# A fused transformer block on one core: the bias add moves to GpSimd, two more sums are kept, some leftover rows are copied side by side, and the order is new

## The chip, the cores and the metric

The kernel runs on one NeuronCore of a Trainium2 chip. The metric is the device time of one execution in microseconds (us). Before the change it is 149.14 us as the median of three runs (148.47 to 150.26).

## What is computed

The reference normalizes x of 2048 rows and 640 columns (bf16) along its columns, sends the result xn through two branches, and adds both to x:

```python
xn = _layernorm(x, axis=-1)
X = rfft2(xn.astype(float32)) * (w_r + 1j * w_i)
y = irfft2(X, s=(S, D)).astype(bfloat16)          # branch A, S = 2048, D = 640
h = gelu(xn @ w1 + b1)                            # w1: 640 x 1536
return x + y + (h @ w2 + b2)                      # w2: 1536 x 640
```

## The kernel before, in words

The rows of x are held as 16 chunks, one row of each group of 16 in each chunk, with 128 partitions and 640 columns a chunk. Everything of the kernel is one function, which registers operations by name with a class `Plan` (line 108 on): each has an engine, the buffers that it reads and writes, and the operations it must follow. The order is not left to a scheduler at run time: a string `ORDER` (line 251 on) lists all 887 operations as `engine:name`, and each engine works through its own part of that list strictly in order. A string `SLOTS` gives every buffer its slot, PSUM banks among them. `Plan.sync` (line 167) then works out which semaphores each operation must wait for. So an operation that waits holds up all that stands behind it on its engine. The five lists are: `sp` (SyncE, which only issues DMAs, transposes by DMA among them), `pe` (TensorE), `act` (ScalarE), `dve` (VectorE) and `pool` (GpSimd). A `gate` in the code concerns only how a list was made; the machine does not wait for it.

The stages and their names (a number behind the letter is a chunk c, a pair of chunks, a group of chunks or a block):

- **Start.** `idle0` are 38 small products on zeros, until the first chunk is there. `st`, `ag`, `ve`, `rs`, `nm` (lines 521 to 553) make statistics and xn of a chunk on VectorE; from chunk 2 on the power of -1/2 (`rs`, line 532) is on GpSimd. `tp` and `tc` transpose the first four chunks by TensorE and a copy, `td` (line 559) the other twelve by DMA. `table0` and `table1` load ScalarE's tables, `b1mm` and `b1cp` turn b1 into a column.
- **First layer of branch B.** `h{block}.{column tile}.{part}` are products of w1 with the transposed xn into PSUM, `ge` the gelu on ScalarE into gT. Chunks go in blocks of 1, 1, 2, 2, 2, 4 and 4.
- **Second layer.** For each chunk, 12 products of 384 columns and 12 of 256 (parts .0, .3, .6, .9). A chunk in `KEEP` (line 246: 1, 2, 4, 5, 7, 8, 10, 11) has them under the name `k`, and `kk` (line 796, VectorE) adds x + b2 and keeps the sum in float32 where the transposed xn lay. The other chunks have them as `l`, which stay in their PSUM bank until the last product of branch A (`fin`, line 803) is added to the same bank. `os` (line 806, VectorE) adds what is kept, or x + b2, and writes the bf16 result, which `out` stores.
- **b2.** `xs` (lines 602 to 608) adds the row b2, copied to all partitions, to x in place, two chunks at a time (`SUMS` = 2, line 245), eight adds of 1280 columns on VectorE. It must follow the normalization of its chunks; `kk` and `os` read its result. The row lies in a buffer that `u` (below) uses later, so each `u` follows all `xs`. The load `bias2` on SP brings it.
- **Branch A on the way in.** `f1` and `f2` (lines 580 and 584) fold the columns of a pair of chunks (even and odd parts) on VectorE, `G` (line 590) is the first step along the rows on TensorE, `gx` its copy to XV. `b0` to `b5` (line 657) are the transform of the columns for a group of 3, 3, 2, 3, 3 and 2 chunks (`GROUPS`); `xb` copies the result out of PSUM. Each `b` takes four PSUM banks, the same four, so b1 waits until both copies of b0 are done. A product here has 160 columns: four with 128 rows for a chunk, and for the 32 leftover rows of each of the four parts four with 32 rows, which use a quarter of the array each (function `width`, line 644).
- **Middle.** `c` (line 722) and `d` (line 731) are the second step along the rows and its inverse, in 16 groups of 32 products with 32 rows and columns each; `y` copies, `m` and `z` multiply with the filter W (VectorE), `u` copies to U. `vt` (line 705) are 16 transposes by DMA from U to XV, issued by SP.
- **The way back.** `e0` to `e5` (line 756) are the mirror of b, for the same groups; each reads all 16 transposes' results and the table `i`. Their weights are slices of XV with a step of 16 elements. `yo` copies out, `y2` and `yf` unfold the columns (VectorE), then `fin` and `os`.

In the order before, part .0 to .9 of l3 and the first part of l0 stand between the last d and e0 on TensorE, and the rest of l0 behind e0.

Of the kernel before, what the change touches and what calls it, by code (L numbers as in the profile page):

```python
# [107 lines left out]
class Plan:  # L108
# [58 lines left out]
    def sync(self):  # L167
# [8 lines left out]
        for o in self.ops:  # L176
            o.waits = [d for d in set(o.deps) if d.dma or d.eng != o.eng or o.eng != "pe"]
# [68 lines left out]
KEEP = (1, 2, 4, 5, 7, 8, 10, 11)  # L246
# [5 lines left out]
sp:x0 dve:warm0 act:bias1 pool:id0 pool:wpad dve:eps5 pool:id1 pe:idle0 sp:x1 act:table0 pool:xbpad2a pool:mhalf pool:xbpad0a pool:xbpad0b  # L252
pool:xbpad1b sp:w1_00 pool:xbpad1a pool:xbpad2b sp:w1_01 sp:w1_02 dve:st0.0 sp:x2 dve:st0.1 sp:w1_03 dve:st1.0 sp:w1_04 dve:ag0 dve:st1.1 sp:w1_10
act:sq0 dve:rs0 dve:ag1 sp:w1_11 dve:nm0 act:sq1 pe:b1mm dve:nm0.3 act:table1 sp:w1_12 dve:rs1 pe:tp0.3 dve:nm1 pe:tp0.0 sp:w1_13 pe:idle1 dve:tc0.0
pe:tp1.0 sp:w1_14 dve:f10.1 pe:h0.0.0 dve:f10.0 sp:x4 pe:h0.1.0 act:tc1.0 pe:h0.0.1 pe:h0.1.1 sp:x6 dve:f20.11 pe:h0.0.2 act:tc0.3 dve:f20.00
pe:h0.1.2 pe:h1.1.0 sp:g act:b1cp pe:h1.1.1 pe:h1.1.2 sp:x8 pe:h1.0.0 dve:st3.0 pe:h1.0.1 pe:h1.0.2 sp:x10 dve:st3.1 pe:h0.0.3 pe:h1.0.3 sp:x12
pe:h1.1.3 dve:ag3 dve:st2.0 pe:h0.0.4 pe:h0.1.3 dve:ve3 pe:h1.0.4 act:ge0.1 dve:st2.1 pe:h0.3.0 pool:rs3 pe:h1.1.4 act:ge1.0 pe:h0.2.0 dve:ag2
act:ge0.0 pe:h0.3.1 dve:ve2 pe:h0.1.4 act:ge1.4 dve:nm3 pe:h0.2.1 pool:rs2 pe:h0.2.2 act:ge0.3 dve:f20.10 pe:h1.3.0 act:ge1.1 pe:h1.3.1 dve:f20.01
pe:h0.3.2 act:ge1.2 dve:nm2 pe:tp3.0 pe:h1.3.2 dve:f11.0 pe:h1.3.3 act:tc3.0 pe:h1.3.4 dve:f11.1 pe:h0.3.3 pe:tp2.0 act:ge0.2 dve:st5.0 pe:h0.2.3
pe:h0.2.4 act:tc2.0 pe:h1.2.0 dve:st4.1 pe:h1.2.1 pe:h0.3.4 dve:st4.0 act:ge1.10 pe:h1.2.2 pe:h1.2.3 act:ge0.11 dve:st5.1 pe:h1.2.4 act:ge1.9  # L260
pe:h2.6.0 dve:ag4 act:ge1.5 dve:ag5 pe:h2.6.3 dve:st7.0 act:ge1.7 pe:h2.7.0 act:ge0.9 dve:ve4 dve:f21.10 pe:h2.2.0 pool:rs4 act:ge1.3 dve:f21.01
act:ge1.11 pe:h2.2.3 dve:st6.1 pe:h2.3.0 act:ge0.4 dve:nm4 act:ge0.5 pe:h2.7.3 act:ge0.10 pe:h2.3.3 dve:st7.1 sp:td4 pe:h2.10.0 act:ge1.8 dve:f21.00
act:ge2.6 pe:h2.10.3 pe:h2.11.0 dve:nm5 act:ge2.7 pe:h2.11.3 dve:st9.1 act:ge1.6 pe:h2.0.0 act:ge0.6 sp:td5 dve:st9.0 pe:G1 act:ge2.10 dve:f21.11
# [60 lines left out]
kps5_0:5 kps5_384:7 fps5_0:0 fps5_384:3 yo2:1 y22:0 yf2:0 eps2:0 os6:0 fps6_0:5 fps6_384:4 os7:1 kps7_0:5 kps7_384:7 fps7_0:2 fps7_384:7 yo3:0 y23:0  # L324
yf3:1 eps3:0 os8:0 kps8_0:4 kps8_384:5 fps8_0:5 fps8_384:7 os9:3 fps9_0:5 fps9_384:3 os10:2 kps10_0:7 kps10_384:4 fps10_0:0 fps10_384:2 yo4:1 y24:0
yf4:0 eps4:0 os11:2 kps11_0:4 kps11_384:7 fps11_0:4 fps11_384:4 os12:0 fps12_0:1 fps12_384:2 os13:1 fps13_0:7 fps13_384:0 yo5:1 y25:0 yf5:0 eps5:0
os14:1 fps14_0:6 fps14_384:4 os15:3 fps15_0:1 fps15_320:3 fps15_480:5
"""


def bass_parallel_sum__spectral_gfnet__dense_activation_gelu__prompt_kernel(
# [20 lines left out]
    K = Plan(nc)  # L352
# [494 lines left out]
```

## Time and profile before

| | us |
|---|---|
| median of three runs | 149.14 (148.47 to 150.26) |
| the profiled execution, its own time | 148.87 |
| its span, first to last instruction | 147.5 |
| TensorE busy (of the span) | 141.7 (96%) |
| VectorE busy | 114.7 (78%) |
| ScalarE busy | 79.3 (54%) |
| GpSimd busy | 7.2 (5%) |

A line such as `PE L410` names the engine and the line of the kernel. Here all products of TensorE but the transposes have line 410, and most copies line 420 (ScalarE) or 421 (VectorE), since helpers record them; they are told apart by what they read and write (`ps<-getab,XV` are the e groups, `ps<-EB,XV` the b groups, `ps<-T,ntab` the d groups, `ps<-xnT,W` the first layer, `ps<-W,gT` the second). In a timeline the first number is the start, the second the length of the run of operations, `x` their number, and the bracket the idle time of the engine before it. Operations overlap by some tens of ns at their ends, so the sum of single lengths is more than the length of a run.

### The profile page before, as it was taken

To read this page: it belongs to the slowest core of one execution; us is meant where nothing else is said; L and a number is where in the kernel's file an instruction comes from. 1 tells how busy PE (TensorE), PEld (TensorE's weight loads), DVE (VectorE), ACT (ScalarE), POOL (GpSimd) and SP (SyncE) were. 2 spreads that over 40 slices of the span, in tenths; PEclk is the share of its full clock that TensorE was granted. 3 is DMA by queue.
4 is the path that set the end of the run, shared out by engine and by line. 5 is a ranking of instruction groups with operands and counts; after the bars stand their busy time and mean duration, and the time that the engine had idled before them with its cause. 6 is when DMAs were issued, how large, how long until landed. Compare 5 with 4: busy or idle time off the path is not lost.

```text
span 147.5 us, 4149 instructions
## 1 busy us (share of the span) xinstructions
PE 141.7 (96%) x1751; PEld 99.8 (68%) x1760; DVE 114.7 (78%) x264; ACT 79.3 (54%) x149; POOL 7.2 (5%) x24
## 2 busy tenths in 40 slices
PE   7999999999999999999999999999899999999993
PEld 7899898886478867455364434446686786667882
DVE  2999999999997555798988999410488789296993
ACT  3659998979755734577795767655242102300000
POOL 2030204112000000000000000000000000000000
PEclk9999999999999999999999999999999999999999
DMA  4999869887999899000007685669001022012225
GB/s 135 306 354 408 142 141 343 145 101 137 293 155 160 221 201 266 16 4 0 7 0 57 126 118 99 103 131 94 2 0 49 0 78 102 5 44 89 89 93 178
DMA packets 29226, 18.40 MB, mean 125 GB/s; under 512 B 20248, under 2 KB 27928, under 8 KB 29080
## 3 DMA queue, kind: packets, MB, share of 16 engines
q1 hardware_dynamic: 29184, 18.14, 54.2%
q8 instruction: 14, 0.23, 0.6%
q14 instruction: 4, 0.03, 0.1%
q10 hardware_dynamic: 24, 0.00, 0.0%
HBM read 10.92 MB, written 2.62 MB: 92 GB/s over the span
## 4 chain that ended last, share of the span: by engine, by line
PE 86%; DMA 4%; ACT 3%; DVE 2%; SPq 2%; issue 1%
PE ps L410 85%; DMA XV<-U 2%; SPq L705 2%; ACT Xb L420 2%; DMA X<-in_A_x_dram 2%; DVE U L521 1%; ACT U L420 1%; PE ps L567 1%; ACT gT L639 0%; DVE T L553 0%; DVE W L806 0%; DVE mv L523 0%; DVE rstd L527 0%
## 5 line engine op out<-in xcount | busy, mean ns | idle before, releaser
L410 PE MATMUL ps<-W,gT 128*128 128x256 bf16 (+3 forms) x396 | 59.3, 296 | 0.0
L410 PE MATMUL ps<-xnT,W 128*128 128x256 bf16 (+2 forms) x411 | 55.5, 286 | 1.2 <-issue 1.1
L410 PEld LDWEIGHTS ps<-W,gT 128*128 128x128 bf16 x396 | 36.9, 98 | 15.4 <-issue 1.2
L410 PEld LDWEIGHTS ps<-xnT,W 128*128 128x128 bf16 x420 | 34.5, 98 | 16.0 <-issue 2.8
L639 ACT ACTIVATE gT<-ps,b1col 128x256 bf16<-128x256 f32 (+2 forms) x84 | 37.6, 524 | 10.3 <-PE ps L410 10.0
L420 ACT ACTIVATE Wf<-ps 128x960 bf16<-128x960 f32 (+1 forms) x8 | 6.7, 869 | 19.2 <-PE ps L410 15.7
L521 DVE BATCH_NORM_STATS2 U<-X 128x6 f32<-128x320 bf16 x32 | 14.1, 473 | 2.1 <-DMA X<-in_A_x_dram 2.1
L420 ACT ACTIVATE T<-ps 128x644 bf16<-128x644 f32 (+2 forms) x17 | 9.3, 580 | 4.7 <-PE ps L410 4.7
L796 DVE TENSOR_TENSOR xnT<-ps,X 128x384 f32<-128x384 f32 (+1 forms) x16 | 7.6, 486 | 4.8 <-PE ps L410 4.8
L806 DVE TENSOR_TENSOR W<-ps,xnT 128x384 bf16<-128x384 f32 (+1 forms) x16 | 7.5, 485 | 4.7 <-PE ps L410 4.5
L420 ACT ACTIVATE XV<-ps 128x1280 bf16<-128x1280 f32 (+1 forms) x8 | 9.6, 1202 | 2.0 <-PE ps L410 2.0
L421 DVE CAST Wf<-ps 128x960 bf16<-128x960 f32 (+1 forms) x4 | 4.3, 1073 | 7.1 <-PE ps L410 7.1
L584 DVE TENSOR_TENSOR T<-T 128x128 bf16<-128x128 bf16 (+1 forms) x32 | 8.9, 315 | 0.1
L806 DVE TENSOR_TENSOR W<-ps,X 128x384 bf16<-128x384 f32 (+3 forms) x17 | 7.6, 465 | 1.7 <-PE ps L410 1.6
L410 PE MATMUL ps<-Wf,htab 128*128 128x384 bf16 (+3 forms) x33 | 8.6, 296 | 0.0
L410 PE MATMUL ps<-getab,XV 32*128 32x160 bf16 (+1 forms) x128 | 7.5, 242 | 0.5 <-DMA XV<-U 0.5
L420 ACT ACTIVATE Xb<-ps 128x960 bf16<-128x960 f32 x5 | 6.2, 1260 | 3.4 <-PE ps L410 3.4
L410 PEld LDWEIGHTS ps<-getab,XV 32*128 32x128 bf16 (+1 forms) x128 | 6.7, 146 | 1.7 <-DMA XV<-U 0.8
L420 ACT ACTIVATE U<-ps 128x512 bf16<-128x512 f32 (+2 forms) x13 | 5.3, 475 | 4.4 <-PE ps L410 4.4
L699 DVE TENSOR_TENSOR T<-T 128x644 bf16<-128x644 bf16 x16 | 7.3, 487 | 0.2
L410 PE MATMUL ps<-EB,XV 32*128 32x160 bf16 (+1 forms) x128 | 7.2, 232 | 0.2 <-ACT Xb L420 0.2
L532 POOL TENSOR_TENSOR rstd<-ve,mhalf 128x2 f32<-128x2 f32 (+1 forms) x8 | 6.1, 758 | 26.6 <-DVE ve L531 26.6
(56 smaller groups left out, 124.6 us busy)
## 6 DMA issues: line engine op xcount, KB each, us to landing
out_dram<-W SPq DMA_DIRECT2D x15, 160.0 KB, 1.8
X<-in_A_x_dram SPq DMA_DIRECT2D x7, 320.0 KB, 5.8
W<-in_B_w_dram SPq DMA_DIRECT2D x10, 192.0 KB, 4.7
W<-in_B_w_dram SPq DMA_DIRECT2D x2, 960.0 KB, 7.0
Wf<-in_A_w_r_dram SPq DMA_DIRECT2D x7, 160.5 KB, 5.5
Wf<-in_A_w_i_dram SPq DMA_DIRECT2D x7, 160.5 KB, 3.8
gtab<-c_G SPq DMA_DIRECT2D x1, 512.0 KB, 7.5
htab<-c_H SPq DMA_DIRECT2D x1, 512.0 KB, 6.1
```

The costliest lines, as they stand in the source:

```text
L410: ins = e.matmul(o_, lhsT=lw, rhs=rh, start=st, stop=sp_, skip_group_check=True)
L420: return e.activation(dst(), src(), ACT.Copy)
L421: return e.tensor_copy(dst(), src())
L521: K.op(f"st{c}.{h}", "dve", lambda e, _, c=c, h=h: e.bn_stats(stats[:, c, 6 * h:6 * h + 6], view(X, c * D + H2 * h, [[1, H2]])), reads=[B_ ...
L532: K.op(f"rs{c0}", "pool", lambda e, _, a=a, b=b: e.tensor_tensor(out=rstd[:, a:b], in0=ve[:, a:b], in1=mhalf[:, a:b], op=ALU.pow), reads=[ ...
L567: ins = e.transpose(psb(tps.slot, [[1, 512]]).bitcast(BF)[:, 128 * j:128 * j + 128], xnv(n, 128 * j, [[1, 128]]), ident)
L584: ring_ops.append(K.op(f"f2{pair}.{k}{i}", "dve", lambda e, _, op=op, x1v=x1v, xfv=xfv, o_=o_, o0=o0, o1=o1, w=w: e.tensor_tensor(out=xfv( ...
L639: K.op(f"ge{bi}.{fc}", "act", lambda e, _, c0=c0, nt=nt, fc=fc, f0=f0, hps=hps: e.activation(gT[:, fc, 128 * c0:128 * (c0 + nt)], psb(hps. ...
L699: return e.tensor_tensor(out=rows, in0=rows, in1=view(TT, TB.slot * 4 * KP + r * KP, [[2 * KP, 2], [1, KP]]), op=op)
L705: K.op(f"vt{q}", "sp", lambda e, _, q=q, qq=qq, U=Us[pair]: e.dma_start_transpose(XV[:, :, 128 * q:128 * q + 128], uv(U, D * qq, [[1, D]]) ...
L796: K.op(f"kk{c}.{o0}", "dve", lambda e, _, kps=kps, c=c, home=home, o0=o0, w=w: e.tensor_tensor(out=home[:, o0 // 128:(o0 + w) // 128], in0 ...
L806: K.op(f"os{c}.{o0}", "dve", lambda e, _, c=c, os_=os_, fps=fps, o0=o0, w=w, kept=kept, home=home if kept else None: e.tensor_tensor(out=( ...
```

## The change

Five things are edited.

1. The eight `xs` are given to GpSimd instead of VectorE.
2. `KEEP` becomes (1, 2, 4, 5, 7, 8, 10, 11, 0, 3). The sums of chunks 0 and 3 are kept where w1 lay, which is free after the whole first layer. Their 16 `l` operations become `k`, and four `kk` are added.
3. For the groups 2 to 5 of the way back, `xr` copies the leftover rows of a group from XV (step 16) to T, chunk by chunk side by side, and the products with 32 rows of that group take their weights from there. There are four such copies, xr2, xr3 and xr4 on ScalarE and xr5 on VectorE.
4. An operation no longer waits on a semaphore for a table load of its own engine.
5. `ORDER` and `SLOTS` are new throughout.

```diff
-            o.waits = [d for d in set(o.deps) if d.dma or d.eng != o.eng or o.eng != "pe"]
+            o.waits = [d for d in set(o.deps) if d.dma or d.eng != o.eng or o.eng != "pe" and d.name[:5] != "table"]
...
 SUMS = 2
-KEEP = (1, 2, 4, 5, 7, 8, 10, 11)
+NEAR = (2, 3, 4, 5)
+KEEP = (1, 2, 4, 5, 7, 8, 10, 11, 0, 3)
...
-            xs_ops.append(K.op(f"xs{a}", "dve", lambda e, _, a=a: e.tensor_tensor(
+            xs_ops.append(K.op(f"xs{a}", "pool", lambda e, _, a=a: e.tensor_tensor(
...
+            xr = K.buf(f"xr{gi}", p_xr) if gi in NEAR else None
+            if xr:
+                K.op(f"xr{gi}", "act dve", copy(lambda c0=c0, n=n, xr=xr: view(TT, 384 * xr.slot, [[128, n], [1, 128]]),
+                     lambda c0=c0, n=n: view(XV, 2048 * 4 + c0, [[1, n], [16, 128]])), reads=B_v, writes=[xr])
-                eps_.slot, n, lambda i, g, p0, k: part(XV, p0, k, 2048 * g + c0 + i, [[16, 128]]), getab),
-                reads=B_v + [B_ge], writes=[eps_])
+                eps_.slot, n, lambda i, g, p0, k: part(TT, p0, k, 384 * xr.slot + 128 * i, [[1, 128]]) if xr and g == 4 else part(XV, p0, k, 2048 * g + c0 + i, [[16, 128]]), getab),
+                reads=B_v + [B_ge] + ([xr] if xr else []), writes=[eps_])
```

Of the new order, three stretches matter for what follows. At the start, ScalarE's list is `table0 sq0 sq1 table1 b1cp tc1.0 tc0.3` (before: `... table1 tc1.0 tc0.3 b1cp`). Around the adds on GpSimd:

```
... dve:nm14 sp:W01n dve:ve12 pe:h5.0.3 dve:f25.01 pool:rs12 dve:f25.00 ... dve:nm13 dve:nm12 ... dve:f16.0 dve:f16.1 ... dve:f26.11
dve:f26.10 pe:G10 dve:nm15 pool:xs0 ... dve:f26.01 pool:xs2 dve:f26.00 ... dve:f17.0 ... pe:G12 dve:kk1.0 pe:G13 ... dve:f17.1 ...
pool:xs14 dve:f27.01 ... dve:f27.00 ... dve:f27.11 ... dve:f27.10 ... pe:G15 act:ge4.1 pe:G14 ... pool:xs4 ... pe:b0 ... pool:xs6
dve:kk4.384 ... act:xb0.1 dve:xb0.0 ... pe:b1 pool:xs12 ... pool:xs10 ... pool:xs8 ...
```

And from the last d group to e3 (TensorE, ScalarE, VectorE, and the last transposes of SP):

```
pe:d3.0 act:ge6.4 pe:k3.0.0 dve:u7.0 pe:k3.0.3 dve:u6.0 pe:k3.0.6 sp:vt14 pe:k3.0.9 pe:k0.384.0 dve:kk3.0 pe:k0.0.0 sp:vt13 pe:k0.384.3
pe:k0.384.6 pe:k8.384.0 sp:vt15 pe:k8.384.3 pe:k8.384.6 pe:k0.0.3 pe:k11.0.0 sp:vt12 pe:k8.384.9 pe:k11.0.3 dve:kk8.384 pe:k0.0.6
pe:k11.0.6 pe:k11.0.9 act:xr2 pe:k0.0.9 dve:kk11.0 act:xr3 pe:k3.384.0 dve:kk0.0 pe:k3.384.3 pe:e0 pe:k3.384.6 dve:yo0.1 act:yo0.0
pe:l6.0.0 pe:l6.0.3 dve:y20.0 pe:e1 dve:y20.1 pe:l6.0.6 dve:yf0.1 act:yo1.0 dve:yf0.0 pe:l13.0.0 act:yo1.1 pe:l13.0.3 dve:xr5
pe:l13.0.6 pe:k3.384.9 dve:y21.0 pe:e2 dve:kk3.384 pe:fin1.0 act:yo2.1 dve:yo2.0 pe:k0.384.9 pe:l6.0.9 act:xr4 dve:y21.1 pe:e3
```

Some copies change between ScalarE and VectorE with the order, among them yo3.0 and yo4.1 (to ScalarE) and u7.0 and u6.0 (to VectorE). The load `i` of the way back's table moves into the list of the transposes `vt`, ahead of the last eight of them.

More of the change, by code (lines that the diff above doesn't have):

```diff
@@ new lines @@
+pe:k3.0.0 dve:u7.0 pe:k3.0.3 dve:u6.0 pe:k3.0.6 sp:vt14 pe:k3.0.9 pe:k0.384.0 dve:kk3.0 pe:k0.0.0 sp:vt13 pe:k0.384.3 pe:k0.384.6 pe:k8.384.0 sp:vt15
+pe:k8.384.3 pe:k8.384.6 pe:k0.0.3 pe:k11.0.0 sp:vt12 pe:k8.384.9 pe:k11.0.3 dve:kk8.384 pe:k0.0.6 pe:k11.0.6 pe:k11.0.9 act:xr2 pe:k0.0.9 dve:kk11.0
+act:xr3 pe:k3.384.0 dve:kk0.0 pe:k3.384.3 pe:e0 pe:k3.384.6 dve:yo0.1 act:yo0.0 pe:l6.0.0 pe:l6.0.3 dve:y20.0 pe:e1 dve:y20.1 pe:l6.0.6 dve:yf0.1
+act:yo1.0 dve:yf0.0 pe:l13.0.0 act:yo1.1 pe:l13.0.3 dve:xr5 pe:l13.0.6 pe:k3.384.9 dve:y21.0 pe:e2 dve:kk3.384 pe:fin1.0 act:yo2.1 dve:yo2.0
@@ new lines @@
+kps4_384:4 fps4_0:3 fps4_384:5 os5:1 kps5_0:5 kps5_384:4 fps5_0:3 fps5_384:1 yo2:0 y22:0 yf2:0 eps2:0 xr2:2 os6:2 fps6_0:5 fps6_384:2 os7:0 kps7_0:4
+kps7_384:5 fps7_0:7 fps7_384:0 yo3:1 y23:0 yf3:1 eps3:0 xr3:0 os8:0 kps8_0:6 kps8_384:7 fps8_0:6 fps8_384:2 os9:3 fps9_0:3 fps9_384:0 os10:2 kps10_0:7
+kps10_384:4 fps10_0:6 fps10_384:1 yo4:0 y24:0 yf4:0 eps4:0 xr4:2 os11:1 kps11_0:5 kps11_384:4 fps11_0:2 fps11_384:2 os12:3 fps12_0:7 fps12_384:1
+os13:2 fps13_0:6 fps13_384:5 yo5:0 y25:0 yf5:0 eps5:0 xr5:1 os14:1 fps14_0:4 fps14_384:7 os15:2 fps15_0:5 fps15_320:1 fps15_480:4
```

144 lines of the change are left out of this document (68 added, 76 removed).

## The prediction

> **What bounds the kernel now.** I read the first part of the page, then the chain that ended last, then busy time by stage, then the timelines of the single engines.
>
> ```profile
> span 147.5 us, 4149 instructions
> PE 141.7 (96%) x1751; PEld 99.8 (68%) x1760; DVE 114.7 (78%) x264; ACT 79.3 (54%) x149; POOL 7.2 (5%) x24
> ```
> ```profile
> 6.53:60.00 53.47, 53.42 (x632) 42.85 (x632) 46.71 (x131) 40.11 (x84) 6.06 (x8) 1.00 0.94 218
> 60.00:95.00 35.00, 33.56 (x636) 16.58 (x640) 31.41 (x54) 24.83 (x46) 0.15 (x2) 1.00 0.34 50
> 95.00:104.00 9.00, 8.49 (x79) 4.63 (x49) 0.56 (x1) 4.52 (x9) 0.00 (x0) 1.00 0.76 109
> 104.00:145.00 41.00, 40.97 (x389) 30.86 (x389) 32.03 (x64) 6.74 (x8) 0.00 (x0) 1.00 0.15 54
> ```
>
> The columns of the second view are the stretch, its length, then busy time of TensorE, its weight loads, VectorE, ScalarE and GpSimd, then the granted clock (1.00 throughout), DMA share and GB/s. From 6.53 us, where the first layer begins, to 145, TensorE is idle for 0.05 + 1.44 + 0.51 + 0.03 = 2.03 us. The matrix work is the same before and after, but for the weight loads of the four copied groups, so a new order can win **at most 2.0 us**. What lies before 6.53 (load and normalize the first chunk) and after 145 (the last add and its store) stays as it is.
>
> ```profile
> 95.37 1.42 ACT U L420 x4
> 98.89 1.26 SPq L705
> 100.19 3.65 DMA XV<-U
> 103.89 41.09 PE ps L410 x375
> L421 DVE CAST U<-ps 128x512 bf16<-128x512 f32 x2 | 1.4, 692 | 0.5 <-PE ps L410 0.5
> ```
>
> The first four rows are the chain, the last a group. The chain shows the 0.51: the last transposes of stage d set the start of `e0`. Then TensorE alone sets 41 us.
>
> **The change, part by part.** The sum is made against the profiled execution, 148.87 us; the median of the three runs, 149.14, stands 0.27 above it.
>
> *Cover for the transposes.* From d3.0 to e0, the sum over the order list (spacing times count, spacing from rows such as the 15 matmuls of 256 columns from 45.54 to 47.17 and the 18 of 384 from 111.38 to 114.32 below, so 0.109 and 0.163) is 8.1 us of matmuls before and 8.8 after: chunks 0 and 3 now lie there as kept sums, with k11.0. The chain wants about 1.0 from the end of `d3.0` to a finished U7 (VectorE, 0.69 for the piece of 512 and 0.28 for that of 128; two such pairs took ScalarE 1.42), then four issues on SP, 1.30 apart (98.89 to 100.19), of which three lie before the last one begins, and 3.65 for that one: 1.0 + 3.9 + 3.65 = 8.6. The load `i` that now stands among the transposes goes out before the last eight and delays nothing of this. So the wait goes: **-0.5 us**. With 0.7 us less cover, as before, it is back.
>
> *Openings of banks.* In the middle TensorE pays extra where a matmul that opens a new bank follows a group of 32-row tiles:
>
> ```profile
> 45.54 1.80 PE L410 MATMUL ps<-xnT,W 128*128 128x256 bf16 x15
> 47.17 0.72 PE L410 MATMUL ps<-gtab,T 128*128 128x128 bf16 x10
> 51.73 1.31 PE L410 MATMUL ps<-EB,XV 128*128 128x160 bf16 x24
> 52.98 1.80 PE L410 MATMUL ps<-W,gT 128*128 128x384 bf16 x12
> 60.93 1.03 PE L410 MATMUL ps<-xnT,W 128*128 128x512 bf16 x4 [0.16 <-issue]
> 67.19 1.32 PE L410 MATMUL ps<-EB,XV 128*128 128x160 bf16 x24 [0.21 <-ACT Xb L420]
> 106.72 1.36 PE L410 MATMUL ps<-getab,XV 128*128 128x160 bf16 x24
> 108.01 1.49 PE L410 MATMUL ps<-W,gT 128*128 128x256 bf16 x12
> 111.38 3.10 PE L410 MATMUL ps<-W,gT 128*128 128x384 bf16 x18
> 114.32 0.33 PE L410 MATMUL ps<-Wf,htab 128*128 128x384 bf16 x1
> ```
>
> The row at 60.93 stands for seven such in that view, six of them behind a c or d group. In the old order 13 of the 16 c and d groups are followed by an opening, in the new one 8. If as large a part of them pays, 6 x 8/13 is 3.7, so 2.3 fewer at 0.16: **-0.4 us** (bounds: 0, and 7 x 0.16 = 1.1).
>
> *Leftover rows side by side.* A group of three chunks on the way back takes 108.01 - 106.72 = 1.29 us, the same shapes on the way in, whose leftover rows lie side by side already, 52.98 - 51.73 = 1.25. I take 0.045 for each of four groups: **-0.2 us**. The copies on ScalarE (xr2, xr3) wait for the same transposes as `e0`:
>
> ```profile
> L420 ACT ACTIVATE T<-ps 128x512 bf16<-128x512 f32 x4 | 2.4, 598 | 1.1 <-PE ps L410 1.1
> L420 ACT ACTIVATE U<-ps 128x128 bf16<-128x128 f32 x6 | 1.7, 281 | 0.0
> 105.36 0.97 ACT L420 ACTIVATE Wf<-ps 128x960 bf16<-128x960 f32 x1 [3.49 <-PE ps L410]
> 105.36 1.16 DVE L421 CAST Wf<-ps 128x960 bf16<-128x960 f32 x1 [6.75 <-PE ps L410]
> ```
>
> Between the first two rows 256 and 384 columns come to 0.39 and 0.49, together 0.88, beside `e0`'s own 1.35 (103.89 to 105.24): hidden. At twice that, as the stride of 16 is not in any row, yo0 would be 0.4 late. Queued behind xr2 and xr3 is only yo0.0, and `e1` waits for it. xr5 costs VectorE about 0.4.
>
> *The groups e0 to e3 stand closer.* From e0 to e1 the new order has 1.31 us of matmuls, and the evacuation of e0's banks ends 1.16 + 0.12 after it: no wait to speak of. From e2 to e3 there are 0.98, and VectorE must fit yo2.0 (0.82) behind y21.0 and kk3.384. I charge **+0.2 us**. After that VectorE is less pressed than now: it is busy 32.0 of 41 us from 104, and loses yo3.0 and yo4.1 to ScalarE (about 1.2 each) while it gains two halves of kept sums (0.42 each) and xr5.
>
> *Head.* `b1cp` now goes ahead of `tc1.0` on ScalarE:
>
> ```profile
> 6.67 0.98 ACT L420 ACTIVATE xnT<-ps 128x640 bf16<-128x640 bf16 x2
> 7.53 0.19 ACT L510 ACTIVATE b1col<-ps 128x12 f32<-128x12 f32 x1
> ```
>
> tc1.0 ends 0.1 later, and h1.1.0 needs it: **+0.1 us**. The dropped wait of ScalarE on its own table loads costs and wins nothing: ScalarE works in order, and the first reader of each table waits for VectorE or TensorE anyway.
>
> *The eight adds move to GpSimd.* VectorE loses 8 x 0.82 us:
>
> ```profile
> L604 DVE TENSOR_TENSOR X<-X,U 128x1280 bf16<-128x1280 bf16 x8 | 6.2, 820 | 0.0
> 37.47 2.29 DVE L604 TENSOR_TENSOR X<-X,U 128x1280 bf16<-128x1280 bf16 x3
> 40.01 1.56 DVE L604 TENSOR_TENSOR X<-X,U 128x1280 bf16<-128x1280 bf16 x2
> 43.48 1.02 DVE L584 TENSOR_TENSOR T<-T 128x512 bf16<-128x512 bf16 x4
> ```
>
> Five of them (2.29 + 1.56) and a sixth, together about 4.5 us as they overlap a little, lie before the last fold, which ends at 43.48 + 1.02 = 44.50. Without them, and with kk1.0 (0.5) ahead, it ends near 40.5. The new order calls for it 3.25 us of matmuls earlier (42.28 against 45.53 ahead of the last pair of G), at 47.17 - 3.25 = 43.9. So VectorE has 3.4 us to spare there. What does an add take on GpSimd? No row has it. Nearest are
>
> ```profile
> 1.17 0.29 POOL L428 TENSOR_SCALAR_AFFINE_SELECT EB<-EB 128x128 bf16<-128x128 bf16 x1 [0.20 <-POOL EB L427]
> 1.50 0.11 POOL L437 MEMSET Xb<- 128x9 bf16 x1
> ```
>
> which give (0.29 - 0.11)/119 = 1.5 ns an element with one operand, so 2.0 us for 1280; with the second operand read at the same rate 3.9. I take the middle, 2.9, and keep 2.0 and 3.9 (VectorE's own 0.82 would be the least). [...] The first add waits for b2:
>
> ```profile
> 32.85 0.60 SPq L405 DMA_DIRECT2D U<-in_B_b_dram  x1
> U<-in_B_b_dram SPq DMA_DIRECT2D x1, 160.0 KB, 4.0
> L421 DVE CAST Xb<-ps 128x960 bf16<-128x960 f32 x3 | 3.7, 1249 | 3.7 <-PE ps L410 3.7
> ```
>
> With the load about where it was, the adds start at 36.9. The fourth, xs4, ends at 36.9 + 4 x 2.9 = 48.5. kk4.384 on VectorE waits for it (0.42, done 48.9), and queued behind kk4.384 stands xb0.0 (1.25, done 50.15), for which `b1` waits. b1 has 1.47 us of matmuls less ahead of it than before: 51.73 - 1.47 = 50.3. It just fits, so the adds are hidden: **0**. Without that cover, at 3.9, xs4 ends at 52.5 and b1 starts 3.9 late.
>
> **The sum**: 148.87 - 0.5 - 0.4 - 0.2 + 0.2 + 0.1 + 0 = **148.1 us**, with 147.0 to 149.3 for this case (openings 0 to 1.1, up to 1 us of new waits).
>
> **The rivals.** *GpSimd and VectorE stop each other.* GpSimd's small operations show a wait on VectorE:
>
> ```profile
> 23.91 0.89 DVE L580 TENSOR_TENSOR T<-T 128x640 bf16<-128x640 bf16 x2
> 24.04 0.91 POOL L532 TENSOR_TENSOR rstd<-ve,mhalf 128x2 f32<-128x2 f32 x1 [1.20 <-DVE ve L531]
> 27.40 0.69 POOL L532 TENSOR_TENSOR rstd<-ve,mhalf 128x2 f32<-128x2 f32 x1 [2.45 <-DVE ve L531]
> 27.22 0.49 DVE L521 BATCH_NORM_STATS2 U<-X 128x6 f32<-128x320 bf16 x1
> ```
>
> Beside a fold of VectorE with two operands in SBUF the operation takes 0.91, beside statistics with one 0.69. If a long add on GpSimd holds up VectorE in the same way, each fold behind it waits for its end. Speaking against it: the second fold of the row at 23.91 runs inside the GpSimd operation and isn't longer (0.89 for two of 0.48, which overlap). But those operations have two elements, ours 1280. The price: six adds come between VectorE's folds before the last one is done, so it ends at 40.5 + 6 x 2.0 = 52.5, 8.6 after the G that needs it, and TensorE, in order, stands: 148.1 + 8.6 = **156.7 us**; at 2.9 an add 162. It begins to decide at two stops (4.0 against 3.4 spare).
>
> [...]
>
> *The add is at the slow end.* At 3.9 us, b1 is 3.9 late: **152.0 us**. For it: GpSimd has one operand at 1.5 ns an element already. Against: 2.9 just fits.
>
> *The order takes nearly all the idle time.* 2.0 of waits and 0.2 of weight loads go and nothing new comes: 148.87 - 2.2 = **146.7 us**. For it: VectorE's load falls in every stage. Against: 1.1 of the 2.0 are openings, which stay in part.
>
> *The waits only change places*: the transposes are covered, and e1 to e3 and the openings take it back: 148.9 us.
>
> **How the numbers follow.** A measurement of this kernel can tell about 1% from no change, so faster is below 147.4 and slower above 150.4 on the profiled scale. Forecast 0.42 (0.10 of it below 147.4), nearly all the idle time 0.12, waits change places 0.06, slow adds 0.12, GpSimd and VectorE stop each other 0.28, as the lengthened GpSimd rows are for it and the fold's row against. That makes faster 0.10 + 0.12 = 0.22, same 0.32 + 0.06 = 0.38, slower 0.12 + 0.28 = 0.40. The range 146.6 to 157.5 leaves out the dearer half of the stops and little below.
>
> **What would show it.** Right: no wait on `DMA XV<-U` in the chain, the adds on GpSimd under 3 us each, VectorE's folds of line 584 still at 0.41, some five rows of `0.16 <-issue`. Wrong: folds or G groups of TensorE waiting between 38 and 56 us (the stops); kk4.384 waiting for POOL with b1 idle behind it (slow adds); waits before e1 to e3.

## The result, and the profile after

The changed kernel takes **167.75 us** (median of 5 runs, 166.76 to 168.5) against 149.14 (five runs, 148.47 to 150.28): a ratio of **1.125, 95% interval 1.121 to 1.129**. The forecast was 148.1 and its range ended at 157.5: wrong, and on the side of the first rival, beyond its price of 156.7 and of 162. The profiled execution took 168.5, its span is 167.2.

The head of the page of the changed kernel, with TensorE's share and the rows in 40 slices:

```profile
span 167.2 us, 4172 instructions
PE 146.0 (87%) x1760; PEld 100.9 (60%) x1760; DVE 128.1 (77%) x260; ACT 82.1 (49%) x153; POOL 28.8 (17%) x32
PE   7999978699670009999999999999999999999994
POOL 2032013024999990000000000000000000000000
PEclk9999999999999555899999999999999999999999
```

VectorE has eight adds less and is busy 13.4 us more (128.1 against 114.7). A slice is 4.2 us. GpSimd is full in slices 11 to 15; TensorE stands still in 13 to 15, and its clock is at half in 14 to 16. The stop in one place, by the timelines of GpSimd, VectorE and TensorE of the changed kernel:

```profile
40.78 21.51 POOL L605 TENSOR_TENSOR X<-X,U 128x1280 bf16<-128x1280 bf16 x8 [2.44 <-DMA U<-in_B_b_dram]
```
```profile
40.15 0.56 DVE L585 TENSOR_TENSOR T<-T 128x128 bf16<-128x128 bf16 x2
...
40.98 5.38 DVE L585 TENSOR_TENSOR T<-T 128x128 bf16<-128x128 bf16 x2
46.40 2.78 DVE L581 TENSOR_TENSOR T<-T 128x640 bf16<-128x640 bf16 x1
49.10 0.55 DVE L801 TENSOR_TENSOR xnT<-ps,X 128x384 f32<-128x384 f32 x1
49.57 2.42 DVE L581 TENSOR_TENSOR T<-T 128x640 bf16<-128x640 bf16 x1
52.02 10.55 DVE L585 TENSOR_TENSOR T<-T 128x128 bf16<-128x128 bf16 x4
```
```profile
62.63 1.25 PE L411 MATMUL ps<-gtab,T 128*128 128x128 bf16 x10 [13.11 <-DVE T L585]
```

Read the second fence against the first. Two folds take 0.56 us at 40.15, ahead of the first add. From 40.78 on a fold takes 2.4 to 2.8 us, its wait included, as long as one add: eight adds, eight folds, one let through between two adds. The last add ends at 62.29, the last fold at 62.57, and the last pair of G waits 13.1 us for it. Only `kk1.0` (49.10) keeps its time in the middle of this: 0.55. It too is a TENSOR_TENSOR, but one of its operands comes from PSUM. Two groups of the changed kernel, the adds and the folds of 512 columns (busy time, mean ns of one):

```profile
L605 POOL TENSOR_TENSOR X<-X,U 128x1280 bf16<-128x1280 bf16 x8 | 21.5, 2722 | 2.4 <-DMA U<-in_B_b_dram 2.4
L585 DVE TENSOR_TENSOR T<-T 128x512 bf16<-128x512 bf16 x16 | 13.8, 865 | 0.0
```

An add takes 2.72 us. The 16 folds of 512 columns take 865 ns in the mean, where the rows of the prediction had 1.02 us for four folds of both widths: the mean hides a few folds of 2.7 us among many of 0.41, and only the timeline shows which.

The rest of the bill, from the stretches (stretch, length, busy time of TensorE, weight loads, VectorE, ScalarE, GpSimd, then the clock) of the changed kernel:

```profile
20.00:45.00 25.00, 20.77 (x184) 15.44 (x183) 23.63 (x71) 19.46 (x36) 8.27 (x7) 1.00 0.94 185
...
60.00:75.00 15.00, 12.37 (x141) 8.88 (x142) 5.49 (x4) 6.11 (x9) 2.29 (x1) 0.73 0.07 26
75.00:110.00 35.00, 35.00 (x590) 18.29 (x575) 28.84 (x47) 20.60 (x36) 0.14 (x2) 1.00 0.15 31
122.00:165.00 43.00, 42.80 (x408) 32.05 (x405) 31.88 (x68) 10.86 (x13) 0.00 (x0) 1.00 0.22 67
```
```profile
54.00:55.00 1.00, 0.00 (x0) 0.00 (x0) 1.00 (x2) 0.00 (x0) 1.00 (x2) 0.67 0.74 191
...
67.00:68.00 1.00, 1.00 (x7) 0.69 (x6) 0.00 (x0) 0.25 (x1) 0.00 (x0) 0.50 0.00 0
```
```profile
PE ps L411 <- DVE T L585: 13.6, 2, 13.1
PE ps L411 <- DMA W<-in_B_w_dram: 3.4, 2, 2.0
```

Three things besides the 13.6 us. The clock is at half from 54.3 (0.67 in the mean of 54 to 55) to 68, so the products from 62.6 on, 5.4 us of them, cost **2.7** too much. TensorE waits **3.4** for the two halves of w2, where it waited for none before. And it idles **less** later: nothing from 75 to 110 and 0.2 from 122 to 165, where the stretches of before showed some 2 us. Of these, 1.1 are the seven waits ahead of openings, which are not won by the order, as the section on the prediction shows.

### The profile page after: what moved, and what is told of

It is laid out like the page before. It is cut to its first block, busy times and chain, and to the rows that moved or that the text cites. A ratio compares the mean times of both kernels' runs of the same rounds, so it can differ in the third digit from the quotient of the medians.

```text
span 167.2 us, 4172 instructions
## 1 busy us (share of the span) xinstructions
PE 146.0 (87%) x1760; PEld 100.9 (60%) x1760; DVE 128.1 (77%) x260; ACT 82.1 (49%) x153; POOL 28.8 (17%) x32
## 4 chain that ended last, share of the span: by engine, by line
PE 61%; DVE 14%; POOL 9%; DMA 7%; SPq 6%; issue 1%
PE ps L411 61%; POOL X L605 8%; DVE T L585 6%; DVE U L522 4%; DMA X<-in_A_x_dram 4%; SPq L406 4%; DMA U<-in_B_b_dram 3%; SPq L560 3%; DVE T L554 2%; POOL rstd L533 1%; DVE T L581 1%; DVE mv L524 0%; DVE ve L532 0%; DVE W L811 0%
## 5 line engine op out<-in xcount | busy, mean ns | idle before, releaser
L411 PE MATMUL ps<-xnT,W 128*128 128x256 bf16 (+2 forms) x420 | 59.5, 293 | 0.8 <-DMA xnT<-T 0.8
L585 DVE TENSOR_TENSOR T<-T 128x512 bf16<-128x512 bf16 (+1 forms) x32 | 23.3, 761 | 0.1
L605 POOL TENSOR_TENSOR X<-X,U 128x1280 bf16<-128x1280 bf16 x8 | 21.5, 2722 | 2.4 <-DMA U<-in_B_b_dram 2.4
L421 ACT ACTIVATE XV<-ps 128x1280 bf16<-128x1280 f32 (+2 forms) x9 | 10.1, 1138 | 16.8 <-PE ps L411 16.8
L411 PE MATMUL ps<-gtab,T 128*128 128x128 bf16 x80 | 6.5, 230 | 13.6 <-DVE T L585 13.6
L411 PEld LDWEIGHTS ps<-gtab,T 128*128 128x128 bf16 x80 | 5.5, 103 | 14.8 <-DVE T L585 13.4
L581 DVE TENSOR_TENSOR T<-T 128x640 bf16<-128x640 bf16 x16 | 11.6, 744 | 0.1
L422 DVE CAST T<-ps 128x644 bf16<-128x644 f32 x9 | 7.3, 825 | 3.4 <-PE ps L411 3.4
L554 DVE TENSOR_SCALAR T<-X,mv,rstd 128x640 bf16<-128x640 bf16 (+2 forms) x17 | 7.1, 431 | 1.4 <-POOL rstd L533 1.2
L769 DVE TENSOR_TENSOR Wf<-Wf 128x960 bf16<-128x960 bf16 (+1 forms) x12 | 6.9, 596 | 1.2 <-ACT Wf L421 1.0
```

The lines of the kernel that those rows point to most:

```text
L411: ins = e.matmul(o_, lhsT=lw, rhs=rh, start=st, stop=sp_, skip_group_check=True)
L421: return e.activation(dst(), src(), ACT.Copy)
L422: return e.tensor_copy(dst(), src())
L554: norm = K.op(f"nm{c}" if not a else f"nm{c}.3", "dve", lambda e, _, c=c, n=n, a=a, b=b, xnv=xnv: e.tensor_scalar(out=xnv(n, a, [[1, b - a ...
L581: K.op(f"f1{pair}.{k}", "dve", lambda e, _, k=k, op=op, xnv=xnv, x1v=x1v: e.tensor_tensor(out=x1v(H2 * k, [[D, 2], [1, H2]]), in0=xnv(0, 0 ...
L585: ring_ops.append(K.op(f"f2{pair}.{k}{i}", "dve", lambda e, _, op=op, x1v=x1v, xfv=xfv, o_=o_, o0=o0, o1=o1, w=w: e.tensor_tensor(out=xfv( ...
```

## The experiments

Each ratio is to the kernel before, in runs on the same chip, with its 95% interval.

### The adds back on VectorE

```diff
-            xs_ops.append(K.op(f"xs{a}", "pool", lambda e, _, a=a: e.tensor_tensor(
+            xs_ops.append(K.op(f"xs{a}", "dve", lambda e, _, a=a: e.tensor_tensor(
```

> The changed kernel with its eight adds of b2 back on VectorE, at the same places of the same order; all other edits stay. Theory S (GpSimd's adds and VectorE's two-operand folds stop each other): the 18.6 us vanish nearly whole, 147.5 to 151; the folds of the pairs of chunks last 0.41 and 0.48 again and the last pair of G does not wait for VectorE. What remains above 147 are the waits for w2 (2.0 and 1.4 us in the changed kernel's profile), if they come from the order. Rival O (the new order itself puts the folds too late): 155 or more, with G still waiting for folds of normal length. Rival R (GpSimd's reads slow VectorE in proportion): as theory S here.

Measured: 151.29 us, 1.009 (1.005 to 1.013), just above the 151 of theory S. So of the 12.5% the adds on GpSimd are 11.6%, and everything else in the change together is 0.9% **slower** than before, not 0.5% faster. Its folds of 512 columns (busy time, mean ns of one), its longest wait, then stretches of 1 us with the clock as the third last number:

```profile
L585 DVE TENSOR_TENSOR T<-T 128x512 bf16<-128x512 bf16 x16 | 6.5, 413 | 0.0
```
```profile
43.50 1.70 PE L411 MATMUL ps<-W,gT 128*128 128x384 bf16 x6 [2.85 <-DMA W<-in_B_w_dram]
```
```profile
43.00:44.00 1.00, 0.50 (x3) 0.31 (x4) 0.00 (x0) 0.00 (x0) 0.00 (x0) 0.98 1.17 143
44.00:45.00 1.00, 1.00 (x6) 0.46 (x4) 0.00 (x0) 0.00 (x0) 0.00 (x0) 0.50 1.29 175
...
47.00:48.00 1.00, 1.00 (x9) 0.82 (x8) 1.00 (x5) 0.54 (x1) 0.00 (x0) 0.81 0.75 101
```

A fold of 512 columns is back to 0.41 (865 ns in the mean before), and no G waits for a fold. In this execution, of 152.45 us, the wait for w2's second half is dearer than its 2.85 us: behind it the clock is at half from 43.96 to about 47.4, another 1.7. The other six executions of this kernel had a mean clock of 1.00 and took 150.4 to 152.78, so the half clock is not what they lose against before.

### The old order, the adds on GpSimd

```diff
-dve:xs4 dve:xs14 dve:xs8 dve:xs12 dve:xs0 dve:xs6 dve:xs2 dve:xs10
+pool:xs4 pool:xs14 pool:xs8 pool:xs12 pool:xs0 pool:xs6 pool:xs2 pool:xs10
```

(only the names that change, in their places of the old order; the engine in the call of line 604 changes with them)

> The kernel before with one edit: its eight adds of b2 run on GpSimd, the order list is the old one. Theory S: b2 lands near 36.9, eight folds are then still to come and each lets one add of 2.7 us by, so the last fold ends near 37 + 8 x 2.7 = 59 instead of 44.5, the last pair of G (due at 45.5) waits some 13 us, TensorE then runs for some us at a lower clock: 160 to 167. Rival O: within 2 us of 149.1, as the order is the old one. Rival R: as theory S.

Measured: 162.31 us, 1.083 (1.078 to 1.088). The order isn't needed for the stops. Here it is not G that stands longest but the products that need the bank which `kk1.0` empties, since `kk1.0` is queued on VectorE behind the folds. The adds, two rows of folds beside them, and TensorE's waits of this kernel (total, times, longest), in an execution of 166.74 us, the longest of four:

```profile
37.33 21.74 POOL L604 TENSOR_TENSOR X<-X,U 128x1280 bf16<-128x1280 bf16 x8 [2.93 <-DMA U<-in_B_b_dram]
```
```profile
37.22 8.29 DVE L584 TENSOR_TENSOR T<-T 128x128 bf16<-128x128 bf16 x4
...
51.16 8.12 DVE L584 TENSOR_TENSOR T<-T 128x512 bf16<-128x512 bf16 x4
```
```profile
PE ps L410 <- DVE xnT L796: 10.7, 1, 10.7
PE ps L410 <- DVE T L584: 1.8, 1, 1.8
```

### Sixteen adds of half the length

```diff
-SUMS = 2
+SUMS = 1
```

with `pool:xs0` to `pool:xs15`, each pair where the one stood.

> The changed kernel with sixteen adds of 640 columns on GpSimd instead of eight of 1280 (SUMS = 1), each pair at the place of the old one. Theory S with a lock that is held for a whole instruction, and one fold let through between two adds: an add takes about 1.4 us, each fold that runs meanwhile about 1.4 instead of 2.7, so nine folds end 9 x 1.3 = 12 us earlier than 62.6 less what they would have taken, near 54; the last pair of G waits about 4 to 5 us instead of 13.1, less clock is lost: 156 to 160. Rival R (throttled in proportion, no lock for an instruction): a fold takes the same 2.4 to 2.8 us whatever the length of the add beside it, and the time stays at 166 to 169.

Measured: 159.99 us, 1.068 (1.064 to 1.073). The adds and VectorE beside them, in an execution of 161.78 us:

```profile
39.22 22.96 POOL L604 TENSOR_TENSOR X<-X,U 128x640 bf16<-128x640 bf16 x16 [1.75 <-DMA U<-in_B_b_dram]
```
```profile
42.17 1.51 DVE L553 TENSOR_SCALAR T<-X,mv,rstd 128x640 bf16<-128x640 bf16 x1
43.60 2.96 DVE L584 TENSOR_TENSOR T<-T 128x128 bf16<-128x128 bf16 x2
...
48.09 0.54 DVE L800 TENSOR_TENSOR xnT<-ps,X 128x384 f32<-128x384 f32 x1
```

GpSimd's own time is hardly changed (23.0 against 21.5 us), a fold now takes 1.5 us (2.96 for two). A fold's length follows the length of the add beside it (2.4 to 2.8 us beside adds of 2.72, 1.5 beside adds of 1.47): it is shut out for an instruction, not slowed down, and rival R falls. The row at 42.17 was in no theory: a normalization (TENSOR_SCALAR, one operand in SBUF), 0.44 elsewhere, takes 1.51 here, so it is shut out too.

### Fills instead of adds

```diff
-            xs_ops.append(K.op(f"xs{a}", "pool", lambda e, _, a=a: e.tensor_tensor(
-                out=view(X, a * D, [[D, SUMS], [1, D]]), in0=view(X, ...), in1=view(b2bc, ...), op=ALU.add),
+            xs_ops.append(K.op(f"xs{a}", "pool", lambda e, _, a=a: e.memset(
+                view(X, a * D, [[D, SUMS], [1, D]]), 0.0),
```

> The changed kernel with GpSimd's eight adds replaced by eight fills of the same 1280 columns with zero: GpSimd then only writes to SBUF and reads nothing. This leaves x and b2 out of the sum that is stored. How long a fill takes no run shows; the fill of 9 columns took 0.11 us, so anything from 0.3 to 2 us. [...] If any long GpSimd instruction stops VectorE's two-operand instructions, each fold beside a fill lasts about as long as the fill: at 1 us, nine folds take 5 us more and the time is 153 to 156.

Measured: 152.07 us, 1.010 (1.005 to 1.015), as with the adds back on VectorE. GpSimd's row and VectorE's beside it:

```profile
39.09 9.09 POOL L605 MEMSET X<- 128x1280 bf16 x8 [2.01 <-DMA U<-in_B_b_dram]
```
```profile
39.37 1.07 DVE L554 TENSOR_SCALAR T<-X,mv,rstd 128x640 bf16<-128x640 bf16 x1
...
44.53 0.48 DVE L581 TENSOR_TENSOR T<-T 128x640 bf16<-128x640 bf16 x1
45.04 1.03 DVE L585 TENSOR_TENSOR T<-T 128x128 bf16<-128x128 bf16 x4
```

Eight fills of 1.18 us run from 39.09 to 48.2, and the folds beside them keep 0.48 for 640 columns and 1.03 for four. So not every long GpSimd instruction shuts out the folds: an add that reads two operands did (2.4 to 2.8 us a fold), a fill that writes as many columns and **reads** none did not. The normalization at 39.37 takes 1.07 instead of 0.44 all the same; it is the only one beside a fill.

### Work for TensorE during the wait

```diff
+        idle("idle2", 210)
...
-pe:G15
+pe:idle2 pe:G15
```

> The changed kernel with 210 products on zeros (128 columns each, into a bank that nothing reads) on TensorE directly ahead of the last pair of G, so that it works through most of the 13 us in which it now waits for the folds. At 0.054 to 0.07 us each they take 11.3 to 14.7 us, so the last pair of G starts between 62.6 and 64.5. Theory C (the lower clock after the wait, 0.50 from 55 to 68, comes from TensorE having stood idle): the clock stays at 1.00 behind the last pair of G, and the 2.65 us that the products lose there come back: 164.3 to 166.5 against 167.75. Rival (the lower clock comes from load on the other engines or the DMAs at that time, not from idleness): the clock falls all the same, 167.5 to 170.

Measured: 166.04 us (median of four, 163.04 to 168.3, too wide for a ratio); profiled execution 164.51, span 163.2. TensorE's rows, then the stretches with the clock:

```profile
49.53 11.89 PE L411 MATMUL ps<-EB 128*128 128x128 bf16 x210
61.26 0.72 PE L411 MATMUL ps<-gtab,T 128*128 128x128 bf16 x10
```
```profile
49.00:63.00 14.00, 13.95 (x232) 13.35 (x231) 11.83 (x5) 1.82 (x4) 14.00 (x6) 1.00 0.96 182
63.00:75.00 12.00, 12.00 (x181) 8.70 (x179) 6.32 (x9) 5.02 (x8) 0.33 (x1) 1.00 0.02 4
```

In this execution the clock stays at 1.00 through the stall and behind it, with GpSimd and the DMAs no less busy from 49 to 63 than in the changed kernel (14.00 us and a share of 0.96, against 13.29 and 0.82): the ten products of G take 0.72 instead of 1.25. The span is 4.0 us shorter, 1.4 of it since the last pair of G starts earlier (at 61.26 instead of 62.63; the last fold ended at 60.86) and the other 2.6 about what the half clock cost. So theory C holds for this execution: load alone did not lower the clock. The fillers did not keep it up every time: another execution had 1.00 too (163.04 us), but two had a mean clock of 0.98 (167.57 and 168.3). No trace of these is kept, and which of their waits brought the clock down stays open.

### The adds behind the folds

```diff
-                reads=[B_b2b] + B_x[a:a + SUMS], writes=[bs], after=sum(norm_ops[a:a + SUMS], []), ...
+                reads=[B_b2b] + B_x[a:a + SUMS], writes=[bs], after=[all f27] + sum(norm_ops[a:a + SUMS], []), ...
...
+pool:xs0 pool:xs4 dve:kk1.0 pool:xs2 pool:xs6 pool:xs8 pool:xs12 pool:xs10 pool:xs14
```

(this row stands behind the last fold, `f27.10`, and the old places are gone)

> The changed kernel, adds still on GpSimd, but they wait for the last fold of the last pair (near 42 us), in the order of their readers (chunks 0, 4, 2, 6, 8, 12, 10, 14), and kk1.0 stands behind the last fold. Theory S: no fold is beside an add, so none is lengthened; the adds run from about 42 to 64; kk, xb and y read at most one operand from SBUF and keep their durations; kk4.384 waits for the second add until about 47.5, in time for b1: 147.5 to 151, about as e1_adds_back or up to 1 us less. Should multiplies with W (two operands in SBUF) begin before 64, the first ones take 2.7 us each and the time is up to 3 us more. Rival O: 155 or more.

Measured: 152.16 us, 1.017 (1.014 to 1.020), above the range named. TensorE's wait for w2 in this kernel (total, times, longest):

```profile
PE ps L411 <- DMA W<-in_B_w_dram: 2.6, 2, 2.3
```

The adds run from 45.13 on, 20.56 us together, and nothing waits for GpSimd but `kk1.0` (2.7 us, beside TensorE's work). The wait that stands out is again one for w2, here for its first half, with half clock behind it (31.8 to 35.2). Three of the six executions had that lower clock (152.15 to 152.73), three had 1.00 (151.5 to 152.55), so it is at most a part of the loss.

### w2 earlier on SP

SyncE's part of the order alone:

```diff
-sp:td5 sp:x14 sp:W12n sp:w2_0 ... sp:td8 sp:W10m sp:bias2 sp:w2_1 sp:W03p sp:m sp:W00n ...
+sp:td5 sp:x14 sp:w2_0 sp:W12n ... sp:td10 sp:w2_1 sp:td8 sp:W10m sp:bias2 sp:W03p ... sp:td15 sp:m sp:W00n ...
```

> e1_adds_back (adds on VectorE) with another order of loads on SP alone: w2_0 ahead of W12n, w2_1 behind td10 instead of behind bias2, and m, W00n, W11n, n, W03n and W00p behind the last transposes td15 instead of ahead of td13. Theory D (what e1_adds_back still loses against the kernel before is the wait for w2's second half, 2.85 us, and the half clock of some 4 us that follows it, 1.9 us): both go, 146.0 to 148.0, below the kernel before. Rival (the loads only crowd each other; another one is late instead, a transposed chunk for the h4 or h5 group or a filter row): 149 to 152.

> e5_adds_after_folds (adds on GpSimd, behind the last fold) with the order of loads on SP of e7_w2_early. Theory D: the 2.33 us for w2 and the half clock behind them go, 146.0 to 148.5, and the adds on GpSimd cost nothing against e7_w2_early but win nothing either, since TensorE sets the time: within 0.7 us of it. Rival: b2 or the first adds are late for kk4.384 and b1 waits behind it: 1 to 3 us above e7_w2_early.

Measured: 152.67 (1.014, 1.009 to 1.020) and 153.71 (1.025, 1.020 to 1.031). Theory D fell. Its rival held in kind, if the time is above its 152: the waits for w2 shrink to 0.93 and none, and TensorE stands just as long in front of a transposed chunk. TensorE in the first of the two kernels, in an execution of 153.4 us:

```profile
29.21 0.65 PE L410 MATMUL ps<-W,gT 128*128 128x384 bf16 x3 [0.93 <-DMA W<-in_B_w_dram]
38.28 1.44 PE L410 MATMUL ps<-xnT,W 128*128 128x512 bf16 x4 [2.79 <-issue]
```

The profile names no releaser for the second wait; the products behind it are the first on four transposed chunks, the last of which (td8) now stands behind w2's 960 KB on SP. I read it as td8 landing just before TensorE goes on at 38.28, which no row here shows. In the second kernel this wait is 4.56 us, and TensorE goes on at 38.60. Half clock, 3.41 us of it, comes with the wait in both.

In two pairs of kernels that differ in the adds (on VectorE, or on GpSimd behind the folds) the one with GpSimd is slower: 1.017 against 1.009, and here 1.025 against 1.014. The adds themselves don't show as the cause: they start at 45.13 and 46.59, behind all these waits, and only `kk1.0` waits for them. Where the difference comes from stays open.

### w2's products later on TensorE

TensorE's part of the order alone:

```diff
-pe:G4 pe:k1.0.0 pe:h3.11.3 pe:k1.0.3 pe:h3.6.0 pe:h3.6.3 pe:h3.7.0 pe:h3.7.3
+pe:G4 pe:h3.11.3 pe:h3.6.0 pe:h3.6.3 pe:h3.7.0 pe:h3.7.3 pe:k1.0.0 pe:k1.0.3
...
-pe:h5.3.3 pe:k1.0.6 pe:k1.0.9 pe:G12 pe:G13 pe:h4.2.0 ... pe:h4.1.3
+pe:h5.3.3 pe:G12 pe:G13 pe:h4.2.0 ... pe:h4.1.3 pe:k1.0.6 pe:k1.0.9
```

> e1_adds_back (adds on VectorE, the order of loads on SP as in the changed kernel), with the first kept sum later on TensorE: k1.0.0 and k1.0.3 behind h3.7.3 instead of ahead of h3.11.3 (about 1.3 us later), k1.0.6 and k1.0.9 behind h4.1.3 instead of ahead of G12 (about 2.7 us later), kk1.0 behind them. Theory W (the rest of the loss is that the new order asks for the two halves of w2 before they can have landed beside the transposes and the other loads): the waits for w2 fall below 1 us together, the clock stays at 1.00, and the time is 146.5 to 148.6, 0.5 to 2% below the kernel before. Rival (between 20 and 45 us the DMA engines are full, so that whatever TensorE is given next waits for its own transfer): another wait of 1 to 3 us appears at a transposed chunk, and the time stays at 150 to 153.

> e5_adds_after_folds (adds on GpSimd, behind the last fold) with the products k1.0.0 to k1.0.9 moved as in e9_k1_later. Theory W: 146.5 to 148.6; against e9_k1_later within 0.5 us, since VectorE's 6.6 us less lie beside TensorE. Rival: as there, 150 to 153, or kk4.384 waits for its add (second on GpSimd, about 5.4 us behind the last fold) and b1 behind it, 1 to 2 us above e9_k1_later.

Measured: 150.19 (1.0044, 1.0010 to 1.0078) and 149.92 (1.0044, 1.0015 to 1.0074). Half of what theory W promised: the long wait and the half clock are gone, and the time still isn't below that of before, nor in the range of theory W (146.5 to 148.6). In this pair the adds on GpSimd, behind the folds, cost nothing and win nothing. The stretches of before, those of the first of the two kernels, and its TensorE's waits:

```profile
20.00:45.00 25.00, 24.95 (x219) 18.64 (x219) 24.78 (x78) 20.46 (x39) 4.00 (x5) 1.00 0.95 197
...
60.00:100.00 40.00, 38.51 (x660) 19.03 (x666) 31.96 (x55) 27.78 (x53) 0.15 (x2) 1.00 0.38 60
100.00:144.00 44.00, 43.55 (x402) 32.28 (x401) 31.25 (x62) 8.31 (x11) 0.00 (x0) 1.00 0.21 53
```
```profile
20.00:45.00 25.00, 22.66 (x204) 16.89 (x204) 23.31 (x76) 20.24 (x36) 4.05 (x5) 1.00 0.97 181
...
60.00:100.00 40.00, 38.78 (x643) 19.65 (x650) 32.14 (x54) 28.43 (x53) 0.14 (x2) 1.00 0.32 63
100.00:144.00 44.00, 44.00 (x432) 32.17 (x431) 31.81 (x67) 11.73 (x15) 0.00 (x0) 1.00 0.26 67
```
```profile
PE ps L410 <- issue: 1.1, 7, 0.2
...
PE ps L410 <- DMA xnT<-T: 0.8, 1, 0.8
PE ps L410 <- DMA W<-in_B_w_dram: 0.6, 1, 0.6
PE ps L410 <- ACT XV L420: 0.6, 1, 0.6
```

This is the account of the new order without stops: 2.34 us of idle time between 20 and 45 where the old order has 0.05, against 0.27 and 0.45 won later. The 2.34 are now several short waits, on a transposed chunk, on w2 and on a copy of G, none above 0.8.

### Fewer loads beside the transposes

```diff
-sp:W03p sp:m sp:W00n sp:W00m sp:e sp:W01n sp:W11n sp:n sp:W03n sp:W00p sp:td13 sp:td12 sp:td14 sp:td15
+sp:W03p sp:W00m sp:e sp:W01n sp:td13 sp:td12 sp:td14 sp:td15 sp:m sp:W00n sp:W11n sp:n sp:W03n sp:W00p
```

> e9_k1_later with one edit: the loads m, W00n, W11n, n, W03n and W00p stand on SP behind the last transposes (td15) instead of ahead of td13, so that 0.75 MB less is under way beside the second half of w2 and the transposes; w2 itself is not moved. e9_k1_later idles 2.3 us on TensorE between 20 and 45 us, the kernel before 0.05. Theory L (these loads crowd the transposes and w2): the idle time there falls to 1.3 us or less, 148.0 to 149.4. Rival O (the new order of the products and folds asks for chunks earlier than statistics, folds and transposes can give them, whatever else is loaded): it stays at 2 to 2.6 us and the time at 149.5 to 150.7; W00p or n late for the middle stage would show as a wait of VectorE or TensorE behind 60 us and cost more.

Measured: 149.80 us, 0.9995 (0.996 to 1.003). Not told apart by the time: it is inside rival O's range, but the ratio is better than that of the kernel it changes (1.0044 on another chip). The profiled execution, at 150.96 one of the longer ones, still idles 2.38 us between 20 and 45, where theory L wanted 1.3 or less.

### The kernel before with more cover for the transposes

```diff
-pe:l0.0.0 pe:e0 pe:l0.0.3 ... pe:l0.0.9 pe:e1 pe:l0.384.0
+pe:l0.0.0 pe:l0.0.3 pe:e0 ... pe:l0.0.9 pe:l0.384.0 pe:e1
```

> The kernel before with two moves on TensorE and nothing else: l0.0.3 (three products of 384 columns, 0.49 us) goes ahead of e0 instead of behind it, and l0.384.0 (three of 256, 0.33 us) ahead of e1 instead of behind it. Theory T (the wait of e0 for the last transpose, 0.45 to 0.5 us, is short of cover and nothing else): the wait shrinks to 0 to 0.1, e1 still finds its banks free, and the time falls by 0.3 to 0.5 us, a ratio of 0.997 to 0.998, at the edge of what can be measured; the profile shows whether the wait went. Rival (the time comes back at e1, which then waits for the copy of e0 by 0.3 us or more): 0 to 0.2 us, ratio 0.999 to 1.000.

Measured: 149.30 us, 0.997 (0.994 to 1.000), as theory T has it and at the edge of what can be measured: the only kernel here that may beat the one before. Its profile doesn't bear the theory out, though: `e0` still waits 0.36 us (0.45 before), and the last transpose took 3.96 us there (3.65 before).

## Why the prediction was wrong

- **The eight adds move to GpSimd: 0.** This is the step that failed. Duration and cover were worked out each for itself: 2.9 us an add was good (2.72), and VectorE did have time to spare (in the kernel with fills, and with the adds back, no G waits for it). What failed is that the two engines were taken to run side by side, with the folds at 0.22 to 0.48 us. Beside the adds, which read SBUF, each fold, which reads two operands from SBUF, took 2.4 to 2.8 us; the last one ended at 62.57 instead of 40.5, and the last pair of G waited 13.1 us. The adds back on VectorE give 1.009, the adds alone in the old order 1.083, fills that only write 1.010.
- **The chance of 0.28.** The row that spoke against the stop (the second fold at 23.91 inside a GpSimd operation, not longer) was of an operation on two elements, as the text said itself. Why it did not lengthen that fold no run here shows. Evidence from an operation 640 times smaller should not have outweighed the lengthened row. The range, too, ended at 157.5, near the cheap end of this rival.
- **The rival's price, 156.7 to 162.** It counted six stops that start at 36.9. b2 landed at 40.78, so all eight adds still lay ahead of the last fold, which ended at 62.57 instead of 52.5 to 57.9. And it let TensorE go on at full speed after the stall: 2.7 us of half clock were no term at all, nor were 3.4 us of waits for w2.
- **Cover for the transposes, -0.5.** Right: no wait on `DMA XV<-U` in the changed order, and 44.00 of 44.00 us busy from 100 to 144 with w2's products later.
- **Openings of banks, -0.4.** Wrong. The row `issue: 1.1, 7, 0.2` is the same in the new order (in the kernels with fills, with fillers on TensorE, with w2's products later and with fewer loads) as before, though fewer openings stand behind c and d. In the changed kernel itself and in the four kernels that ran together on one chip (adds back, old order, half adds, adds behind the folds) the row is missing, the one with the old order among them: its coming and going has to do with the chip or the execution, not with this order. More the runs don't show.
- **Leftover rows side by side, -0.2.** About half of it, by the rows from one start to the next: the two copied groups of three chunks take 1.31 and 1.25 us in the changed kernel (137.47 - 136.16 and 144.22 - 142.97) against 1.29 before, those of two chunks 0.90 and 0.90 against 0.94 and 0.95. That is 0.1 us in all. No run undid it alone.
- **Closer e groups, +0.2.** Not seen: no wait ahead of e1 to e3.
- **Head, +0.1.** Not seen either: from 6.76 to 20 us TensorE of the changed kernel is busy all the time.
- **What the sum left out.** I looked for new waits where the diff pointed, in the middle and on the way back, and took 20 to 45 us over from before as full. The new order calls for the first products with w2 earlier there, and SP issues thirteen loads between td8 and td13 where eight stood between td11 and td12 before. In the new order without stops this stretch has 2.25 to 4.8 us of idle time, and 1.7 more are lost by the clock where it falls in one piece: more than all that the order wins later. Why it never falls below, whichever transfer is preferred, stays open: the DMA engines are about full there (a share of 0.91 to 1.04 in the kernels of the new order), but the old order has 0.95 as well with 0.05 us of idle time, and the experiment with fewer loads was undecided.

## What to carry to other kernels

Work that is moved to an idle engine is free only if the two engines don't shut each other out (here 13.6 us of waits of TensorE for folds): before a long GpSimd operation that reads SBUF is put beside VectorE, list VectorE's instructions in that stretch by how many operands they read from SBUF, and allow for each two-operand one waiting for a whole GpSimd instruction, as the folds did here (2.4 to 2.8 us beside adds of 2.72). Put it beside instructions that read PSUM, as behind the last fold here: beside eight adds of 2.6 us `kk1.0` kept its 0.56 us, and the copies of 960 columns out of PSUM their 1.25. Price a stall of TensorE with the half clock that can follow it: here 3.41 us of it, a loss of up to 1.7, came with waits of 2.33, 2.79, 2.85 and 4.56 us, and none with waits of 1.83, 2.01 and 2.27. And when an order is new throughout, look for due times of transfers in the stretches that were full before, not only where the idle time was.

## What the runs showed of the hardware

- In the changed kernel GpSimd's adds and VectorE's folds took turns: one fold between two queued adds, eight folds for eight adds at 2.72 us. Adds of half the length (1.47 us) made each stop half as long (1.5 us a fold).
- A one-operand TENSOR_SCALAR of VectorE (bf16, 640 columns, 0.44 us) took 1.51 beside GpSimd's adds of half the length and 1.07 beside a fill, one row of each. A TENSOR_TENSOR with two operands in SBUF was lengthened beside the adds (a fold of 640 columns 2.4 to 2.8 us) and not beside the fills (0.48); one with an operand in PSUM beside neither (0.54 to 0.56).
- TensorE's clock fell to 0.50 some 2.8 to 4.8 us after it began to stand still, also where it was at work again by then, and came back 2.8 to 6 us after work began again. It stayed down for 3.41 us with the adds back (43.96 to 47.37), with the adds behind the folds and in both kernels with w2 earlier, for 6.83 twice with half adds, for 10.24 in the old order (53.02 to 63.26), for 13.65 in the changed kernel: one, two, three and four times 3.41. So waits of 2.33 and of 4.56 us brought the same 3.41 us of half clock; the wait of 2.85 us cost 4.6 with it.
- Waits of 1.83 us (old order, adds on GpSimd), 2.01 (changed kernel) and 2.27 (fillers on TensorE) left the clock at 1.00; waits of 2.33 (adds behind the folds), 2.79 (w2 earlier) and 2.85 (adds back) did not. The length may not be all that decides: in the execution of the old order the mean clock is 0.959 over 165.4 us, by which I estimate 13.6 us of half clock, 3.3 more than the 10.24, and besides its waits of 1.83 and 10.73 the only one of TensorE above 1 us is one of 1.7 for a transpose. No row shows where these 3.3 lay.
- An add of 1280 bf16 columns with two operands took GpSimd 2.60 us in the mean behind the folds and 2.72 to 2.75 beside them, VectorE 0.82; a fill of as many columns took GpSimd 1.18.
